# A fixed order at the start of a fused attention and two-FFN kernel: reciprocals, first weight splits and the last unit placed anew

## The chip, the cores and the metric

The kernel runs on one core of one Trainium2 chip. The metric is the device time of one launch in microseconds (us). Before the change the median of three runs is 981.34 us (981.05 to 982.17).

## The reference

Windowed causal attention with a linear bias per head feeds two feed-forward networks, one with a single input matrix, one gated. All arrays are float32. The sequence is 4 x 576 tokens of 8 heads of 64, so 2304 tokens of 512 features.

```python
def _attn_ref(q, k, v):                  # 4 x 8 x 576 x 64
    scores = scale * np.matmul(q, k.transpose(0, 1, 3, 2))
    rel = pos[:, None] - pos[None, :]
    bias = slopes[:, None, None] * (-np.abs(rel))[None]
    mask = (rel >= 0) & (rel < 128)
    scores = np.where(mask, scores + bias[None], -1e9)
    attn = np.exp(scores - scores.max(-1, keepdims=True))
    return np.matmul(attn / (attn.sum(-1, keepdims=True) + 1e-9), v)

def _moe_ref(x, w_in, w_out):            # 512 -> 2048 -> 512
    h = x @ w_in
    return (h / (1.0 + np.exp(-1.702 * h))) @ w_out

def _moe2_ref(x, w_gate, w_val, w_out):  # 512 -> 1536 -> 512
    g = x @ w_gate
    return (g / (1.0 + np.exp(-g)) * (x @ w_val)) @ w_out
```

## The kernel before, in words

The 2304 tokens are 18 tiles of 128. Attention and the first network take them in five blocks of 4, 3, 4, 3 and 4 tiles (`A_BLOCKS`), the second network in five blocks of 4, 4, 4, 4 and 2. This text calls attention on block 0 the front part; it is the only work there is at the start, and the first network can begin on a head pair of block 0 as soon as that pair's output is there.

**Attention on a block** is eight units: four head pairs `hp`, each in two groups `g` of two query tiles. One unit goes through four steps. `scores` multiplies q and k on TensorE into PSUM tiles `sb`; `fold` (VectorE, L223) moves the masked half of the window into place; four sums on VectorE (L268) add the bias and find the row minimum; four exponentials on ScalarE (ACT, L278) also give the row sums. `norm` turns the row sums into reciprocals on VectorE (L291, L292) and multiplies the four tiles by them on GpSimd (POOL, L294). `transposes` turns the four tiles on TensorE (L327), and the result is copied and masked into `pf`: for the units in `ON_VECTOR` by two VectorE products (L339), for the others by a ScalarE copy (L343) and two GpSimd selects (L344, L347). `values`, once per pair, multiplies `pf` with v into the PSUM tile `xb` (L392) and splits the result into a high part `xh` (ScalarE, L410) and a low part `xl` (VectorE, L411). For block 0 extra matmuls without use (`fill`, L186) stand ahead of the transposes.

**The weights** lie in memory as 64-bit floats. `load_w` loads two chunks of 128 x 512 words each (one of `w_in`, one of `w_out`) into one tile, and `split_w` makes a high and a low float32 part of each in six instructions of 128 x 1024 elements: a ScalarE scaling into `cv` (L155), three VectorE operations on bits (L157, L158, L161), a ScalarE rounding into `wt` (L166) and a VectorE subtraction (L167). The pool `cv` has two buffers. There are 16 such pairs for the first network. The first three are split inside the front part; the others are put ahead of the step that needs them.

**The first network** is `h_part(j, f)` (twelve TensorE matmuls, L416 to L418, three for each of the head pairs 0 to 3 in turn; then tanh on ScalarE, a product `th` on VectorE, `gh` on ScalarE and `gl` on VectorE) and `y_part(j, f)` (another twelve). `h_part(0, 0)` needs only the `w_in` chunk of the first weight pair; `y_part(0, 0)` needs the `w_out` chunk. While block 0 goes through ten of the sixteen `f`, attention on block 1 is placed between.

**What sets the order.** Each engine takes its instructions in the order in which they were placed. In the front part that order is written out by hand: a list `ev` of (time, step), sorted by time, whose steps are placed in that order on VectorE, ScalarE, GpSimd and TensorE (`manual_schedule`). The scores of unit h stand at time h, its `norm` at h + `NORM0`, its transposes at h + `TRANSPOSE0`, and `values` of a pair at its second unit + `VALUES0`; the three steps of weight pair i stand at `SPLITS0[i]`, +1 and +2. Everything after the front part is ordered by a scheduler that goes by its own estimate of the times and may place first-network and block 1 work between steps of the front part.

Of the kernel before, what the change touches and what calls it, by code (L numbers as in the profile page):

```python
# [9 lines left out]
F32R = mybir.dt.float32r  # L10
U32 = mybir.dt.uint32
# [5 lines left out]
P = 128  # L17
# [10 lines left out]
B_BLOCKS = (4, 4, 4, 4, 2)  # L28


NORM0, TRANSPOSE0, VALUES0 = 0.6, 2.2, 5.0

ON_VECTOR = (0, 2, 5)

SPLITS0 = (7, 9, 11)

# [10 lines left out]
def attention_two_ffn(ctx: ExitStack, tc: tile.TileContext, q, k, v, w_in, w_out, w_gate, w_val, w_out2, yscr, out):  # L47
# [92 lines left out]
    def load_w(pool, tag, srcs):  # L140

        t = pool.tile([P, 2, 512, 2], U32, tag=tag, name="wraw")
        for i, src in enumerate(srcs):
            nc.sync.dma_start(out=t[:, i].rearrange("p c w -> p (c w)"), in_=src.bitcast(U32))
        return t, pool, tag

    def split_w(raw):


        words, pool, tag = raw  # L150
        low, high = words[:, :, :, 0], words[:, :, :, 1]
        c = cvp.tile([P, 2, 512], U32, tag="cv", name="cv")
        cf = c.bitcast(F32)

        nc.scalar.activation(out=cf, in_=high.bitcast(F32), func=AF.Abs, scale=REBIAS)  # L155
        yield
        nc.vector.tensor_scalar(out=high, in0=high, scalar1=0x80000000, scalar2=None, op0=ALU.bitwise_and)  # L157
        nc.vector.scalar_tensor_tensor(  # L158
            out=low, in0=low, scalar=29, in1=high, op0=ALU.logical_shift_right, op1=ALU.bitwise_or
        )  # L160
        nc.vector.scalar_tensor_tensor(  # L161
            out=c, in0=c, scalar=3, in1=low, op0=ALU.logical_shift_left, op1=ALU.bitwise_or
        )
        yield
        t = pool.tile([P, 2, 2, 512], F32R, tag=tag, name="wt")
        nc.scalar.activation(out=t[:, :, 0, :], in_=cf, func=AF.Copy)  # L166
        nc.vector.tensor_tensor(out=t[:, :, 1, :], in0=cf, in1=t[:, :, 0, :].bitcast(F32), op=ALU.subtract)  # L167
        yield [t[:, 0], t[:, 1]]

# [64 lines left out]
    def scores(j, hp, g):  # L234


        t0, n, lead = span(j)
        u = units[j, hp]
# [24 lines left out]
        for e in range(2):  # L263
            fold([kind(t0 + i) for i in tiles], sb[e][:, : m * 2 * P], quarters)
        for x in range(2 * m):
            e, i = divmod(x, m)
# [18 lines left out]
            )  # L285
        u["prob", g] = prob, stat

    def norm(j, hp, g):
# [4 lines left out]
        for x in range(m):  # L293
            nc.gpsimd.tensor_scalar(  # L294
                out=prob[:, x],
                in0=prob[:, x],
                scalar1=stat[:, 3, x : x + 1],
                scalar2=1.0,
                op0=ALU.mult,
                op1=ALU.mult,  # L300
            )
# [260 lines left out]
    def split_next(w, raw, upto):  # L562
        for i in range(len(w), min(len(raw), upto)):
            w[i] = list(split_w(raw[i]))[-1]

# [5 lines left out]
    for h in range(H):  # L571
        u = 0, h // 2, h % 2
        ev.append((h, lambda u=u: scores(*u)))
        ev.append((h + NORM0, lambda u=u: norm(*u)))
        ev.append((h + TRANSPOSE0, lambda u=u: transposes(*u)))
        if h % 2:
            ev.append((h + VALUES0, lambda u=u: values(*u[:2])))
    for i, at in enumerate(SPLITS0):
        steps = split_w(raw1[i])

        def step(i=i, steps=steps):
            w1[i] = next(steps)

        ev += [(at + s, step) for s in range(3)]
    E = mybir.EngineType
# [10 lines left out]
    def hooks(j, length):  # L596
# [11 lines left out]
        for h in range(H):  # L608
            u = j, h // 2, h % 2
            ev.append((at + step * h, lambda u=u: (scores(*u), norm(*u))))  # L610
            if h % 2 and h < H - 3:
# [100 lines left out]
```

## Time and profile before

| what | value |
|---|---|
| median of three runs | 981.34 us |
| the profiled execution, its own time | 982.34 us |
| its span in the profile | 980.6 us |
| TensorE matmuls busy | 955.4 us (97% of the span) |
| VectorE busy | 474.8 us (48%) |
| ScalarE busy | 343.6 us (35%) |
| GpSimd busy | 145.9 us (15%) |
| chain that ended last: TensorE / VectorE | 87% / 8% |

The page gives busy time per engine over the whole span, the same in 40 slices of about 24.5 us, and the chain of work that ended last. The shares of the whole say little about a change in the first 60 us; those are read from the stretches of the trace, further down. The profiled execution took 1.0 us more than the median of the runs. Where a tile carries the same name in several blocks (`pf`, `xb`, `sb`), the line tells them apart.

### The profile page before, as it was taken

The numbers are of one execution on the slowest core, as the hardware profiler recorded it, in microseconds if no ns is written. First come the engines' busy times: TensorE is split into PE (matmuls) and PEld (weight loads), VectorE is DVE, ScalarE is ACT, GpSimd is POOL, SyncE is SP. The second block draws the span as 40 slices with busy tenths as digits, with TensorE's granted clock in tenths as the row PEclk, the third lists the DMA queues.
The fourth block names the chain that finished last, engine by engine and source line by source line (L and its number), as shares of the span: only waits on it lengthen the run. The fifth ranks groups of instructions, "written<-read, shape, count | busy, mean of one in ns | idle before, by whom it ended". The sixth has DMA issues, their size and how long they took to land.

```text
span 980.6 us, 13815 instructions
## 1 busy us (share of the span) xinstructions
PE 955.4 (97%) x5358; PEld 790.3 (81%) x5358; DVE 474.8 (48%) x1110; ACT 343.6 (35%) x745; POOL 145.9 (15%) x247
## 2 busy tenths in 40 slices
PE   7798899999999999999999999999999999999998
PEld 5465589987777889898888888888888888888897
DVE  6799882545454335536999722232222222322332
ACT  4566542444344334544655411211121111111211
POOL 4326410332122103420000200200020001000000
PEclk9989999999999999999999999999999999999999
DMA  9912230112311112025556200110011000100010
GB/s 337 337 67 65 92 134 22 49 49 62 93 52 53 36 35 71 15 80 189 193 193 222 79 1 1 44 43 1 1 33 43 1 0 12 43 1 1 6 39 22
DMA packets 30881, 69.05 MB, mean 70 GB/s; under 512 B 3424, under 2 KB 11104, under 8 KB 30816
## 3 DMA queue, kind: packets, MB, share of 16 engines
q1 hardware_dynamic: 30816, 68.17, 20.3%
q8 instruction: 42, 0.69, 0.3%
q14 instruction: 23, 0.19, 0.1%
HBM read 57.67 MB, written 10.49 MB: 70 GB/s over the span
## 4 chain that ended last, share of the span: by engine, by line
PE 87%; DVE 8%; ACT 2%; issue 1%; DMA 1%; POOL 1%; ACTq 0%; POOLq 0%; DVEq 0%
PE hp L416 6%; PE y L416 6%; PE y L418 6%; PE y L417 6%; PE hp L418 6%; PE hp L417 6%; PE pg L416 5%; PE pg L418 5%; PE o L526 5%; PE pv L416 5%; PE o L528 5%; PE pv L418 5%; PE pg L417 5%; PE pv L417 5%; PE o L527 5%; PE sb L255 2%
## 5 line engine op out<-in xcount | busy, mean ns | idle before, releaser
L508 DVE SCALAR_TENSOR_TENSOR t<-t,pg 128x512 f32<-128x512 f32 (+1 forms) x60 | 38.1, 634 | 198.1 <-ACT t L507 198.1
L416 PE MATMUL hp<-xh,wt 128*128 128x512 f32 (+1 forms) x320 | 121.7, 380 | 7.9 <-ACT wt L166 6.4
L417 PE MATMUL y<-gl,wt 128*128 128x512 f32 (+1 forms) x320 | 119.5, 373 | 2.8 <-DVE gl L442 2.8
L418 PE MATMUL y<-gh,wt 128*128 128x512 f32 (+1 forms) x320 | 119.4, 374 | 0.0
L418 PE MATMUL hp<-xh,wt 128*128 128x512 f32 (+1 forms) x320 | 119.0, 372 | 0.0
L417 PE MATMUL hp<-xl,wt 128*128 128x512 f32 (+1 forms) x320 | 119.0, 372 | 0.0
L416 PE MATMUL y<-gh,wt 128*128 128x512 f32 (+1 forms) x320 | 114.1, 380 | 0.2
L507 ACT ACTIVATE t<-pg 128x512 f32<-128x512 f32 (+1 forms) x60 | 33.3, 555 | 196.5 <-PE pg L418 196.5
L294 POOL TENSOR_SCALAR prob<-prob,stat 128x128 f32<-128x128 f32 x144 | 68.8, 496 | 202.0 <-DVE stat L292 154.4
L416 PE MATMUL pg<-yh,wt 128*128 128x512 f32 (+1 forms) x240 | 88.8, 370 | 0.0
L416 PE MATMUL pv<-yh,wt 128*128 128x512 f32 (+1 forms) x240 | 88.6, 369 | 0.0
L418 PE MATMUL pg<-yh,wt 128*128 128x512 f32 (+1 forms) x240 | 88.5, 369 | 0.0
L417 PE MATMUL pg<-yl,wt 128*128 128x512 f32 (+1 forms) x240 | 88.4, 368 | 0.0
L418 PE MATMUL pv<-yh,wt 128*128 128x512 f32 (+1 forms) x240 | 88.4, 368 | 0.0
L417 PE MATMUL pv<-yl,wt 128*128 128x512 f32 (+1 forms) x240 | 88.2, 367 | 0.0
L526 PE MATMUL o<-wt,p2h 128*128 128x512 f32 x216 | 84.7, 392 | 0.0
L528 PE MATMUL o<-wt,p2l 128*128 128x512 f32 x216 | 84.3, 391 | 0.0
L527 PE MATMUL o<-wt,p2h 128*128 128x512 f32 x216 | 84.1, 390 | 0.0
L438 DVE SCALAR_TENSOR_TENSOR th<-th,hp 128x512 f32<-128x512 f32 (+1 forms) x80 | 50.3, 631 | 66.3 <-ACT th L437 65.8
L492 POOL TENSOR_TENSOR yl<-yr,yh 128x512 fp32r<-128x512 f32 (+1 forms) x20 | 25.4, 1281 | 376.4 <-ACT yh L491 266.9
L512 ACT ACTIVATE p2h<-t 128x512 fp32r<-128x512 f32 (+1 forms) x60 | 35.3, 588 | 121.0 <-DVE t L511 120.8
L416 PEld LDWEIGHTS hp<-xh,wt 128*128 128x128 f32 x320 | 60.6, 190 | 19.6 <-ACT wt L166 7.5
(80 smaller groups left out, 1663.1 us busy)
## 6 DMA issues: line engine op xcount, KB each, us to landing
wraw<-in_moe_w_out SPq DMA_DIRECT2D x28, 512.0 KB, 5.2
wraw<-in_moe_w_in SPq DMA_DIRECT2D x16, 512.0 KB, 6.7
wraw<-in_moe_w_gate SPq DMA_DIRECT2D x12, 512.0 KB, 4.1
wraw<-in_moe_w_val SPq DMA_DIRECT2D x12, 512.0 KB, 4.6
out<-ob SPq DMA_DIRECT2D x18, 256.0 KB, 2.0
y_scratch<-yt SPq DMA_DIRECT2D x16, 256.0 KB, 2.0
yr<-y_scratch SPq DMA_DIRECT2D x16, 256.0 KB, 2.7
kr<-in_k SPq DMA_DIRECT2D x8, 320.0 KB, 3.2
```

Of the source, the lines that this page charges most:

```text
L294: nc.gpsimd.tensor_scalar(out=prob[:, x], in0=prob[:, x], scalar1=stat[:, 3, x : x + 1], scalar2=1.0, op0=ALU.mult, op1=ALU.mult,)
L416: nc.tensor.matmul(out=out_ap, lhsT=whi, rhs=xhi, start=start, stop=False)
L417: nc.tensor.matmul(out=out_ap, lhsT=whi, rhs=xlo, start=False, stop=False)
L418: nc.tensor.matmul(out=out_ap, lhsT=wlo, rhs=xhi, start=False, stop=stop)
L438: nc.vector.scalar_tensor_tensor(out=th[:, :m], in0=th[:, :m], scalar=1.0, in1=hp[:, :m], op0=ALU.add, op1=ALU.mult)
L492: nc.gpsimd.tensor_tensor(out=yl[:, kk, :m], in0=t[:, :m], in1=yh[:, kk, :m].bitcast(F32), op=ALU.subtract)
L507: nc.scalar.activation(out=th[:, :m], in_=pg[:, :m], func=AF.Tanh, scale=0.5)
L508: nc.vector.scalar_tensor_tensor(out=th[:, :m], in0=th[:, :m], scalar=1.0, in1=pg[:, :m], op0=ALU.add, op1=ALU.mult)
L512: nc.scalar.activation(out=ph[:, :m], in_=th[:, :m], func=AF.Copy)
L526: nc.tensor.matmul(out=o, lhsT=ph[:, c], rhs=w[:, 0, :], start=(f == 0), stop=False)
L527: nc.tensor.matmul(out=o, lhsT=ph[:, c], rhs=w[:, 1, :], start=False, stop=False)
L528: nc.tensor.matmul(out=o, lhsT=pl[:, c], rhs=w[:, 0, :], start=False, stop=(f == NF2 - 1))
```

## The change

Four things change, all of them in the front part.

1. `scores` becomes a generator in two steps: the matmuls and the fold of unit h at time h, its sums and exponentials at h + 0.1. `norm` of unit h moves to h + 1.05, between the two steps of unit h + 1; that of the last unit to 7 + 1.4.
2. The last unit (number 7) is normalised on VectorE instead of GpSimd (`NORM_ON_VECTOR`), and its mask is on VectorE too. In exchange unit 5 goes to ScalarE and GpSimd: `ON_VECTOR` is (0, 2, 7) instead of (0, 2, 5).
3. The weight pair with the tag `w0` (`SINGLES`) is loaded into two tiles of one chunk each, and each chunk is split by instructions of 128 x 512 elements. The tag is used twice, for the first pair of the first network and for the third pair of the second network.
4. `SPLITS0` now gives one time for each of the three steps of every slot.

```diff
-NORM0, TRANSPOSE0, VALUES0 = 0.6, 2.2, 5.0
-ON_VECTOR = (0, 2, 5)
-SPLITS0 = (7, 9, 11)
+TRANSPOSE0, VALUES0 = 2.2, 5.0
+ON_VECTOR, NORM_ON_VECTOR = (0, 2, 7), 7
+SPLITS0 = ((6.5, 8.3, 8.45), (6.6, 9.25, 12.1)), ((8.6, 12.2, 13),), ((12.15, 13.5, 14),)
+SINGLES = ("w0",)
...
+        slots = ((tag, srcs),) if tag not in SINGLES else tuple((f"{tag}.{i}", (src,)) for i, src in enumerate(srcs))
...
-        c = cvp.tile([P, 2, 512], U32, tag="cv", name="cv")
+        c = cvp.tile([P, 2, 512], U32, tag="cv", name="cv")[:, :n]
...
-            nc.gpsimd.tensor_scalar(
+            (nc.vector if j == 0 and 2 * hp + g >= NORM_ON_VECTOR else nc.gpsimd).tensor_scalar(
...
-        ev.append((h, lambda u=u: scores(*u)))
-        ev.append((h + NORM0, lambda u=u: norm(*u)))
+        steps = scores(*u)
+        ev += [(h, lambda steps=steps: next(steps)), (h + 0.1, lambda steps=steps: next(steps))]
+        ev.append((h + (1.05 if h < H - 1 else 1.4), lambda u=u: norm(*u)))
...
-    for i, at in enumerate(SPLITS0):
-        steps = split_w(raw1[i])
-        def step(i=i, steps=steps):
-            w1[i] = next(steps)
-        ev += [(at + s, step) for s in range(3)]
+    for i, times in enumerate(SPLITS0):
+        w1[i] = []
+        for slot, at in zip(raw1[i], times):
+            steps = split_w(slot)
+            def step(i=i, steps=steps):
+                w1[i] += next(steps) or []
+            ev += [(a, step) for a in at]
```

Three places show how the instructions move. The line numbers after the change are 7 to 10 higher.

VectorE at units 0 and 1, before. `stat_163` belongs to unit 0; `sb_190`, `sb_191` and `stat_189` to unit 1.

```order
L268 ISA prob_162,stat_163<-sb_165,bias_68 128x128
L268 ISA stat_163 128x1
L291 TENSOR_SCALAR stat_163<-stat_163 128x4
L292 RECIPROCAL stat_163<-stat_163 128x4
L223 COPY_PREDICATED sb_190<-later_69,sb_190 128x2x128
L223 COPY_PREDICATED sb_191<-later_69,sb_191 128x2x128
L268 ISA prob_188,stat_189<-sb_190,bias_68 128x128
```

The same place after the change. `stat_164` is unit 0's; `sb_185`, `sb_186` and `stat_184` are unit 1's.

```order
L277 ISA prob_163,stat_164<-sb_166,bias_68 128x128
L277 ISA stat_164 128x1
L230 COPY_PREDICATED sb_185<-later_69,sb_185 128x2x128
L230 COPY_PREDICATED sb_186<-later_69,sb_186 128x2x128
L301 TENSOR_SCALAR stat_164<-stat_164 128x4
L302 RECIPROCAL stat_164<-stat_164 128x4
L277 ISA prob_183,stat_184<-sb_185,bias_68 128x128
```

The two reciprocal instructions of unit 0 stand behind the fold of unit 1 instead of ahead of it; so it goes on up to unit 6.

VectorE behind the sums of the last unit, before. The `pf` rows are the masks of unit 5, the first `xl` is that of pair 1, the second that of pair 2.

```order
L339 TENSOR_TENSOR pf<-pt,keep 128x4x128
L339 TENSOR_TENSOR pf<-pt,drop 128x4x128
L291 TENSOR_SCALAR stat<-stat 128x4
L292 RECIPROCAL stat<-stat 128x4
L411 TENSOR_TENSOR xl<-xb,xh 128x512
L157 TENSOR_SCALAR wraw<-wraw 128x1024
L158 SCALAR_TENSOR_TENSOR wraw<-wraw 128x1024
L161 SCALAR_TENSOR_TENSOR cv<-cv,wraw 128x1024
L167 TENSOR_TENSOR wt<-cv,wt 128x2x512
L216 MEMSET sb 64x128
L411 TENSOR_TENSOR xl<-xb,xh 128x512
```

The same place after, from unit 7's reciprocal on (ahead of it stand `xl` of pair 1 and the three bit operations of the first chunk). The `pf` rows are the masks of unit 7, and the `x2` row is `xl` of pairs 2 and 3.

```order
L302 RECIPROCAL stat<-stat 128x4
L304 TENSOR_SCALAR prob<-prob,stat 128x128 x4
L174 TENSOR_TENSOR wt<-cv,wt 128x512
L349 TENSOR_TENSOR pf<-pt,keep 128x4x128
L349 TENSOR_TENSOR pf<-pt,drop 128x4x128
L164 TENSOR_SCALAR wraw<-wraw 128x512
L165 SCALAR_TENSOR_TENSOR wraw<-wraw 128x512
L168 SCALAR_TENSOR_TENSOR cv<-cv,wraw 128x512
L421 TENSOR_TENSOR xl<-xb,xh 128x512 x2
L174 TENSOR_TENSOR wt<-cv,wt 128x512
```

Both halves of the first weight pair and the whole of unit 7 now stand ahead of `xl` of pair 2, and `xl` of pair 3 follows at once, ahead of the second weight pair.

ScalarE at the same place, before. The `prob` rows are the exponentials of units 6 and 7, and the `pf` rows copies of units 4, 6 and 7.

```order
L278 ACTIVATE prob,stat<-prob,stat 128x128 x4
L343 ACTIVATE pf<-pt 128x4x128
L278 ACTIVATE prob,stat<-prob,stat 128x128 x4
L155 ACTIVATE cv<-wraw 128x1024
L410 ACTIVATE xh<-xb 128x512
L343 ACTIVATE pf<-pt 128x4x128
L166 ACTIVATE wt<-cv 128x2x512
```

And after. The `pf` rows are units 4, 5 and 6.

```order
L287 ACTIVATE prob,stat<-prob,stat 128x128 x4
L353 ACTIVATE pf<-pt 128x4x128
L162 ACTIVATE cv<-wraw 128x512 x2
L287 ACTIVATE prob,stat<-prob,stat 128x128 x4
L353 ACTIVATE pf<-pt 128x4x128
L420 ACTIVATE xh<-xb 128x512
L353 ACTIVATE pf<-pt 128x4x128
L173 ACTIVATE wt<-cv 128x512
```

The scaling of both chunks moves ahead of the exponentials of unit 7, and a copy (unit 5) comes between them and `xh` of pair 1.

VectorE at the reciprocals of block 1's last two units, before.

```order
L158 SCALAR_TENSOR_TENSOR wraw<-wraw 128x1024
L167 TENSOR_TENSOR wt<-cv,wt 128x2x512
L291 TENSOR_SCALAR stat<-stat 128x4
L291 TENSOR_SCALAR stat<-stat 128x2
L161 SCALAR_TENSOR_TENSOR cv<-cv,wraw 128x1024
L292 RECIPROCAL stat<-stat 128x4
L292 RECIPROCAL stat<-stat 128x2
L438 SCALAR_TENSOR_TENSOR th<-th,hp 128x512
```

And after.

```order
L302 RECIPROCAL stat<-stat 128x4
L301 TENSOR_SCALAR stat<-stat 128x2
L164 TENSOR_SCALAR wraw<-wraw 128x1024
L168 SCALAR_TENSOR_TENSOR cv<-cv,wraw 128x1024
L302 RECIPROCAL stat<-stat 128x2
L448 SCALAR_TENSOR_TENSOR th<-th,hp 128x512
L165 SCALAR_TENSOR_TENSOR wraw<-wraw 128x1024
L174 TENSOR_TENSOR wt<-cv,wt 128x2x512
```

Over all VectorE rows ahead of the last of these reciprocals, before there are 13 each of L157, L158 and L161 and 12 of L167, all of 128 x 1024. After there are 12, 11, 11 and 10 of that size and two of each in half size. On TensorE the same rows, 412 of them, stand ahead of and up to the last transpose of block 1 before and after.

## Rows read from the trace of the kernel before

**Rows 1.** Stretches: length, busy of PE, PEld, DVE, ACT, POOL, clock, DMA, GB/s.

```profile
0.00:6.12 6.12, 4.54 (x22) 4.14 (x24) 2.13 (x13) 1.28 (x1) 1.46 (x9) 1.00 0.63 197
6.12:31.93 25.81, 21.36 (x148) 13.71 (x146) 19.26 (x108) 14.07 (x63) 12.31 (x31) 1.00 1.02 391
31.93:57.00 25.07, 17.86 (x95) 10.88 (x96) 21.34 (x49) 14.08 (x33) 8.11 (x16) 0.86 0.70 255
57.00:116.77 59.77, 53.33 (x278) 37.61 (x276) 58.88 (x139) 37.24 (x76) 28.53 (x26) 0.91 0.23 69
```

**Rows 2.** Waits of TensorE from 118 us to the end: total, times, longest.

```profile
PE hp L416 <- ACT pf L343: 0.6, 1, 0.6
PE hp L416 <- DVE xl L411: 0.2, 1, 0.2
```

**Rows 3.** Timeline (start, length, instruction [idle before]) at block 1's last units.

```profile
116.56 0.21 DVE L292 RECIPROCAL stat<-stat 128x4 f32<-128x4 f32 x2
...
116.89 2.12 POOL L294 TENSOR_SCALAR prob<-prob,stat 128x128 f32<-128x128 f32 x6 [2.61 <-DVE stat L292]
...
117.32 0.33 PE L327 MATMUL pt<-ident,prob 128*128 128x128 f32 x1 [0.66 <-POOL prob L294]
```

**Rows 4.** Timeline of VectorE in block 0's attention.

```profile
9.31 0.17 DVE L291 TENSOR_SCALAR stat<-stat 128x4 f32<-128x4 f32 x1 [1.08 <-ACT prob L278]
...
24.03 0.08 DVE L268 DVE_READ_ACCUMULATOR2_ANT stat<- 128x1 f32 x1
...
26.22 0.69 DVE L411 TENSOR_TENSOR xl<-xb,xh 128x512 fp32r<-128x512 f32 x1 [0.58 <-ACT xh L410]
...
30.07 0.17 DVE L291 TENSOR_SCALAR stat<-stat 128x4 f32<-128x4 f32 x1 [1.14 <-ACT prob L278]
```

**Rows 5.** Timeline of ScalarE: exponentials of unit 7, scaling, copy, `xh`.

```profile
25.13 0.58 ACT L343 ACTIVATE pf<-pt 128x512 f32<-128x512 f32 x1
25.61 0.58 ACT L410 ACTIVATE xh<-xb 128x512 fp32r<-128x512 f32 x1
...
31.33 0.40 ACT L278 ACTIVATE prob<-prob,stat 128x128 f32<-128x128 f32 x1 [0.82 <-DVE stat L268]
...
32.89 1.13 ACT L155 ACTIVATE cv<-wraw 128x1024 f32<-128x1024 f32 x1
```

**Rows 6.** Timeline of VectorE behind the front part.

```profile
34.53 0.69 DVE L411 TENSOR_TENSOR xl<-xb,xh 128x512 fp32r<-128x512 f32 x1 [0.97 <-ACT xh L410]
35.14 1.18 DVE L157 TENSOR_SCALAR wraw<-wraw 128x1024 uint32<-128x1024 uint32 x1
36.35 1.54 DVE L158 SCALAR_TENSOR_TENSOR wraw<-wraw 128x1024 uint32<-128x1024 uint32 x1
...
43.58 0.68 DVE L157 TENSOR_SCALAR wraw<-wraw 128x1024 uint32<-128x1024 uint32 x1
...
56.10 1.21 DVE L158 SCALAR_TENSOR_TENSOR wraw<-wraw 128x1024 uint32<-128x1024 uint32 x1
57.24 1.21 DVE L167 TENSOR_TENSOR wt<-cv,wt 128x1024 fp32r<-128x1024 f32 x1
```

**Rows 7.** Timeline of TensorE: `values` of pairs 2 and 3, first `hp`, later `hp`.

```profile
35.49 2.17 PE L392 MATMUL xb<-pf,qkv 128*64 128x256 f32 x20
40.29 0.80 PE L416 MATMUL hp<-xh,wt 128*128 128x512 f32 x1 [2.63 <-ACT wt L166]
```

**Rows 8.** VectorE groups by form, 0 to 120 us: busy, mean ns, idle before.

```profile
L442 DVE TENSOR_TENSOR gl<-th,gh 128x512 fp32r<-128x512 f32 x7 | 4.7, 677 | 0.0
...
L115 DVE TENSOR_SCALAR bias<-rel 128x128 bf16<-128x128 f32 x8 | 1.2, 221 | 0.0
...
L108 DVE TENSOR_SCALAR later<-rel 128x128 f32<-128x128 f32 x1 | 0.3, 294 | 0.1
```

**Rows 9.** Stretches around the second fall of TensorE's clock.

```profile
53.90:57.30 3.40, 1.36 (x6) 0.59 (x4) 3.40 (x7) 3.06 (x8) 2.16 (x4) 1.00 0.01 2
57.30:60.70 3.40, 3.40 (x24) 2.73 (x24) 3.40 (x6) 2.54 (x4) 0.26 (x1) 0.50 0.01 2
```

More of the change, by code (lines that the diff above doesn't have):

```diff
@@ L140, in load_w @@
     def load_w(pool, tag, srcs):
[L142 to L145, printed above, removed]
+        slots = ((tag, srcs),) if tag not in SINGLES else tuple((f"{tag}.{i}", (src,)) for i, src in enumerate(srcs))
+        raws = []
+        for tag, srcs in slots:
+            t = pool.tile([P, len(srcs), 512, 2], U32, tag=tag, name="wraw")
+            for i, src in enumerate(srcs):
+                nc.sync.dma_start(out=t[:, i].rearrange("p c w -> p (c w)"), in_=src.bitcast(U32))
+            raws.append((t, pool, tag))
+        return raws
     def split_w(raw):
         words, pool, tag = raw
+        n = words.shape[1]
         low, high = words[:, :, :, 0], words[:, :, :, 1]
-        c = cvp.tile([P, 2, 512], U32, tag="cv", name="cv")
+        c = cvp.tile([P, 2, 512], U32, tag="cv", name="cv")[:, :n]
         cf = c.bitcast(F32)
@@ L164, in split_w @@
         yield
-        t = pool.tile([P, 2, 2, 512], F32R, tag=tag, name="wt")
+        t = pool.tile([P, n, 2, 512], F32R, tag=tag, name="wt")
         nc.scalar.activation(out=t[:, :, 0, :], in_=cf, func=AF.Copy)
         nc.vector.tensor_tensor(out=t[:, :, 1, :], in0=cf, in1=t[:, :, 0, :].bitcast(F32), op=ALU.subtract)
-        yield [t[:, 0], t[:, 1]]
+        yield [t[:, i] for i in range(n)]
     def w1_src(i):
@@ L264, in scores @@
             fold([kind(t0 + i) for i in tiles], sb[e][:, : m * 2 * P], quarters)
+        yield
         for x in range(2 * m):
@@ L286, in scores @@
         u["prob", g] = prob, stat
+        yield
     def norm(j, hp, g):
@@ L563, in split_next @@
         for i in range(len(w), min(len(raw), upto)):
-            w[i] = list(split_w(raw[i]))[-1]
+            w[i] = [chunk for slot in raw[i] for chunk in list(split_w(slot))[-1]]
     for hp in range(H // 2):
@@ L609, in hooks @@
             u = j, h // 2, h % 2
-            ev.append((at + step * h, lambda u=u: (scores(*u), norm(*u))))
+            ev.append((at + step * h, lambda u=u: (list(scores(*u)), norm(*u))))
             if h % 2 and h < H - 3:
```

## Prediction

> **What bounds the kernel now.** I read first where TensorE stops waiting. From 118 us to the end it waits twice, 0.6 and 0.2 us [rows 2], so whatever shifts its work up to there shifts the end by as much. Its last long waits before that end at 117.32, with the transposes of block 1's last units: they waited for GpSimd's six multiplications, which waited for two reciprocals on VectorE, done at 116.77 [rows 3]. The order puts the same 412 TensorE rows up to the last transpose of block 1 before and after, so the work that is left behind is the same. Then I read VectorE up to 116.77, by stretches [rows 1]. It is busy 2.13 + 19.26 + 21.34 + 58.88 = 101.61 us and idle 15.16: 3.99 before the first scores (to 6.12), 6.55 in the front part (6.12 to 31.93, the end of the last unit's sums), 3.73 from there to 57, and 0.89 in the last 59.77. TensorE in that last stretch is busy 53.33 of 59.77, part of it at a clock share below 1 (mean 0.91), so it has room and VectorE has none. So the last reciprocal of block 1 is a sum of two things, the VectorE work that stands ahead of it and the VectorE idle ahead of it, and I cost the change as the change of these two.
>
> **The work ahead of the last reciprocal.** (a) By the order, three instructions of 128 x 1024 no longer stand ahead of it: one L158, one L161, one L167, if two halves count as one. Such an instruction is followed by the next 1.14 us after its start (56.10 to 57.24) [rows 6], so 3 x 1.14 = 3.4 us less. They are only put off: the weights they make belong to a later f of the first network, and VectorE has free time once TensorE sets the pace. (b) Unit 7's four multiplications come to VectorE. No row of before shows that operation there. The nearest from below is L115, one input, 128 wide, 0.221 us; from above L108, 0.294 us with a float32 result [rows 8]. I take 4 x 0.22 = +0.9 (0.6, if the starts are closer than the lengths, to 1.3). That GpSimd loses them gains nothing here, since nothing but unit 7 waits. The masks change places between units 5 and 7, two L339 each, at no net cost. (c) Four VectorE instructions of 1024 become eight of 512. Two of 512 take 2 x 0.677 = 1.35 [rows 8] where one of 1024 takes 1.21 [rows 6], so +0.15 each, +0.6 (0.2 to 0.6). (d) The first weight pair's L157 and L158 took 1.18 and 1.54 where later ones take 0.68 and 1.21 [rows 6], 0.8 more, while GpSimd normalised and masked. The first chunk will still meet GpSimd's masks of units 5 and 6, the second will not: -0.4 (-0.8 to 0). Sum: -3.4 + 0.9 + 0.6 - 0.4 = **-2.3**.
>
> The Trainium skill ("GPSIMD Engine Reference", Key points) says that GpSimd shares its SBUF interfaces with VectorE and contends with VectorE instructions in a two-port mode or with two SBUF inputs; it speaks against moving unit 5's masks to GpSimd beside the first chunk. By it (d) would be 0 and the forecast 0.4 later; the trace agrees as far as the 1.18 against 0.68 goes.
>
> **Idle in the front part.** The 6.55 are six waits, first 1.08, last 1.14 us [rows 4], 5.99 in all, and 0.56 of small gaps. Five are waits for the exponentials, ahead of a reciprocal; the reciprocal now stands behind the next unit's fold. The fold of an even unit takes 1.15 to 1.2 and covers a wait of 1.1; that of an odd one takes 0.64 and leaves about 0.5. Unit 0's and unit 6's waits so become 0.5, unit 1's and 3's vanish. Pair 0's `xl` is not helped: it starts 2.2 us after the sums of unit 5 (24.03 to 26.22) [rows 4], because ScalarE has the exponentials, a copy and `xh` to do [rows 5], in the same order after. VectorE did unit 5's reciprocals in that time and now does not, so 2.2 idle stay. Left are 0.5 + 2.2 + 0.5 + 0.56 = 3.8, so **-2.7** (-3.2 to -2.0). The last sums end at 29.2 instead of 31.93.
>
> **Idle behind it.** Here the new order adds two waits. First, `xl` of pair 1. Counted back from 29.2 (0.84 for the sums, 0.5 wait, 0.3 reciprocals, 0.64 fold, 0.84 sums) unit 6's sums start at 26.1 and its exponentials run from 26.4 to 28.0 (1.6 per unit, 31.33 to 32.89) [rows 5]. In ScalarE's queue then stand a copy (0.5), two half scalings (1.15 for both, by the 1.13 of the whole), the exponentials of unit 7, a copy and `xh` (0.5 each): 28.0 + 0.5 + 1.15 + 1.6 + 0.5 + 0.5 = 32.25, and `xl` starts at 32.35. That is 2.2 ahead of before (34.53 [rows 6]), but VectorE waits 3.1 for it. Queued behind are the first chunk, unit 7's norm and the whole split. Second, `xl` of pair 3. VectorE goes on at 32.95 with the first half (1.55 + 0.2 for GpSimd), reciprocals 0.3, norm 0.9, half `wt` 0.6, masks 1.2, second half 1.55, `xl` of pair 2 0.6, done at 39.85. TensorE turns unit 7 by 36.2, does `values` of pair 2 and the first two of pair 3 in 2.17 [rows 7] (38.4), then, by the order, six `hp` and one pair of scores (about 1.95 at 0.23 each and a few gaps, 40.3), and only then the rest of `values` (1.4, 41.7). ScalarE's `xh` makes it 42.4, and `xl` of pair 3 starts at 42.5: a wait of 2.65. But TensorE sits idle for some 3 us ahead of unit 7. After a stretch with 1.36 of 3.40 us busy its clock fell from 2.4 to 1.2 GHz (share 1.00, then 0.50) and it did 3.4 us of work at half rate [rows 9], which lost 1.7 us. If that happens here the wait is 4.35. I take 3.5, the middle. With 0.3 of small gaps the 3.73 of before become 6.9, so **+3.2** (+2.3 to +5.2). At the end, 0.89 may grow if VectorE now and then comes before TensorE has the input: **+0.2** (-0.3 to +2.5).
>
> TensorE's own start gains: the first `hp` at 38.4 instead of 40.29 [rows 7]. That hides nothing more, since it waits for the second weight pair anyway. On SP only two tags of the same loads change, and the first weights are loaded far ahead of 28 us. The second network's split in halves adds about 0.6 to a VectorE that is half busy over the span, and TensorE does not wait there [rows 2]: nothing, and 0.6 if that cover were gone.
>
> **The sum.** -2.3 - 2.7 + 3.2 + 0.2 = -1.6 us. The profiled execution took 982.34 us around a span of 980.6, so it would take 980.7; the median of the runs is 1.0 lower, and 981.34 - 1.6 gives **979.7 us**. With all bounds together: -3.4 - 3.2 + 2.3 - 0.3 = -4.6, and -1.5 - 2.0 + 5.2 + 2.5 = +4.2. I take 0.2% (1.96 us) as what a measurement of this kernel can tell from no change.
>
> **Rivals.** (1) Slower: TensorE sets the pace of the tail. Unit 7's turn, `values` and the first `hp` run at 1.2 GHz, and on VectorE first `xl` of pair 3 and then `th` of the first `hp` head the queue, so each us of TensorE's lateness is a us of VectorE idle, with the second and third weight pairs behind. Price: +0.85 for the wait of 4.35 instead of 3.5, +2.4 for twelve `hp` at 0.43 instead of 0.23, and +0.9 for half of one more stretch at half rate at the wait for the second weights: -1.6 + 4.15 = +2.55, 983.9 us. It decides as soon as TensorE is more than 1.6 us later than I have it. For it speaks that rows 9 show the fall; against it that the chain gives this stretch to VectorE. The Trainium skill ("TensorE: Matmul & The Clock Gate", What's actually happening) says that the throttled state is the default and that activity releases it; by it the fall ahead of unit 7 is likely, and the trace agrees (1.36 busy of 3.40 us, then 0.50). (2) Faster: the clock holds at 2.4 GHz in the tail (wait 2.65, -0.85) and the first chunk does not collide with GpSimd (-0.4), and the last stretch's small waits vanish (-0.5): -3.3, 978.0 us. For it speaks that short waits in the front part cost no clock (share 1.00) [rows 1]. (3) No gain: the lead is there at 57, but TensorE, 53.33 of 59.77 busy, cannot follow, and VectorE idles until TensorE has its inputs: 0 to -0.6, 981.0 us. Against it speaks the clock share of 0.91 in that stretch, which leaves TensorE room.
>
> **Chances.** The forecast's own case 0.42 (978.3 to 981.1, and about 4 in 10 of it beyond 0.2%), rival 1 0.16, rival 2 0.25, rival 3 0.17. Faster by over 0.2%: 0.42 x 0.4 + 0.25 x 0.95 + a little = 0.42. Slower by over 0.2%: 0.16 x 0.75 = 0.12. Within: 0.46. The range for 8 in 10 is 976.9 to 982.9; the forecast's own is 978.3 to 981.1.
>
> **What the profile will show.** Right: the sums of unit 7 end near 29.2; no wait over 0.6 ahead of a reciprocal in block 0 but for the one at pair 0's `xl` (about 2.2); a VectorE wait of about 3 before `xl` of pair 1 and of 2.6 to 4.4 before that of pair 3; the last reciprocals of block 1 near 115; TensorE's clock at 0.50 once between 33 and 42. Wrong: if VectorE idles over 2 us between 57 and 115 (rival 3), if `th` of the first `hp` is waited for (rival 1), or if TensorE waits somewhere behind block 1's last transpose.

## The result, and the profile after

The changed kernel takes **990.14 us** (median of four runs, 989.42 to 991.47) against 981.75 of the kernel before beside it: ratio 1.0084, 95% interval 1.0071 to 1.0097. I had predicted 979.7 us and a range up to 982.9; the change is slower by 8.4 us. The profiled execution took 990.1 us around a span of 988.4; the span is 7.8 us longer than before. TensorE's matmuls are busy 959.3 us of it, against 955.4 before, for the same work: so about half of the 7.8 us is more idle time on TensorE and half is work done slower (mean granted clock 0.983 against 0.990).

The stretches of after, for [rows 1] (length, busy of PE, PEld, DVE, ACT, POOL, clock, DMA, GB/s):

```profile
0.00:6.12 6.12, 4.54 (x22) 4.14 (x24) 2.13 (x13) 1.28 (x1) 1.45 (x9) 1.00 0.66 188
6.12:31.93 25.81, 22.82 (x150) 15.67 (x148) 18.91 (x107) 15.93 (x69) 13.33 (x34) 0.87 1.02 394
31.93:57.00 25.07, 17.39 (x90) 9.93 (x90) 19.72 (x47) 11.33 (x23) 3.34 (x5) 0.81 0.71 254
57.00:116.77 59.77, 52.38 (x283) 37.50 (x281) 55.34 (x141) 36.60 (x78) 29.32 (x30) 0.94 0.22 70
```

VectorE idles 4.43 us in the last of these stretches (59.77 - 55.34), where it idled 0.89 before; from there to its last reciprocal, at 119.62, it is busy throughout. The timeline of VectorE behind the front part, for [rows 6]:

```profile
33.15 0.69 DVE L421 TENSOR_TENSOR xl<-xb,xh 128x512 fp32r<-128x512 f32 x1 [2.94 <-ACT xh L420]
33.75 0.57 DVE L164 TENSOR_SCALAR wraw<-wraw 128x512 uint32<-128x512 uint32 x1
34.36 1.00 DVE L165 SCALAR_TENSOR_TENSOR wraw<-wraw 128x512 uint32<-128x512 uint32 x1
...
36.32 0.16 DVE L301 TENSOR_SCALAR stat<-stat 128x4 f32<-128x4 f32 x1
...
39.84 0.69 DVE L165 SCALAR_TENSOR_TENSOR wraw<-wraw 128x512 uint32<-128x512 uint32 x1
...
45.70 0.69 DVE L421 TENSOR_TENSOR xl<-xb,xh 128x512 fp32r<-128x512 f32 x1 [3.23 <-ACT xh L420]
...
49.30 0.67 DVE L448 SCALAR_TENSOR_TENSOR th<-th,hp 128x512 f32<-128x512 f32 x1
...
78.55 0.69 DVE L448 SCALAR_TENSOR_TENSOR th<-th,hp 128x512 f32<-128x512 f32 x1 [1.25 <-ACT th L447]
...
107.24 0.23 DVE L230 COPY_PREDICATED sb<-later,sb 128x64 f32<-128x64 uint32 x1 [2.45 <-PE sb L263]
...
117.46 0.16 DVE L302 RECIPROCAL stat<-stat 128x4 f32<-128x4 f32 x1
...
119.47 0.15 DVE L302 RECIPROCAL stat<-stat 128x2 f32<-128x2 f32 x1
```

The two new waits (2.94 and 3.23 us) are there, and block 1's last reciprocals end at 117.62 and 119.62, not near 115 (116.77 before, [rows 3]). Most of the idle time behind 57 us is the wait of 2.45 us for scores of block 1. TensorE's timeline at unit 7, ahead of these scores, and at block 1's last units, where [rows 3] had a wait of 0.66:

```profile
37.06 1.08 PE L337 MATMUL pt<-ident,prob 128*128 128x128 f32 x4 [3.74 <-DVE prob L304]
38.08 3.45 PE L402 MATMUL xb<-pf,qkv 128*64 128x256 f32 x20
...
98.05 1.17 PE L337 MATMUL pt<-ident,prob 128*128 128x128 f32 x3 [1.32 <-POOL prob L304]
100.30 0.47 PE L337 MATMUL pt<-ident,prob 128*128 128x128 f32 x1 [1.08 <-POOL prob L304]
...
106.65 0.54 PE L263 MATMUL sb<-kr,qr 64*64 64x192 f32 x4
...
119.84 0.48 PE L337 MATMUL pt<-ident,prob 128*128 128x128 f32 x1 [2.68 <-POOL prob L304]
...
126.96 0.44 PE L337 MATMUL pt<-ident,prob 128*128 128x128 f32 x2
```

TensorE's clock is at its lower level from 98.8 to 105.6 us, and the twelve `hp` matmuls between the second wait and the scores start 0.43 us apart instead of 0.23. The last of block 1's transposes in the kernel before, which no row ahead shows:

```profile
123.14 0.44 PE L327 MATMUL pt<-ident,prob 128*128 128x128 f32 x2
```

And the waits of TensorE from 118 us to the end, for [rows 2] (total, times, longest):

```profile
PE pt L337 <- POOL prob L304: 2.7, 1, 2.7
PE y L426 <- ACT gh L451: 1.2, 1, 1.2
PE y L427 <- DVE gl L452: 0.6, 1, 0.6
PE hp L426 <- ACT pf L353: 0.6, 1, 0.6
```

The middle two are new: TensorE is starved again behind block 1. The timeline of ScalarE there shows by what:

```profile
136.06 0.62 ACT L451 ACTIVATE gh<-th 128x512 fp32r<-128x512 f32 x1
140.91 1.12 ACT L162 ACTIVATE cv<-wraw 128x1024 f32<-128x1024 f32 x1 [4.23 <-DMA wraw<-in_moe_w_out]
141.93 1.05 ACT L173 ACTIVATE wt<-cv 128x1024 fp32r<-128x1024 f32 x1
143.24 0.90 ACT L447 ACTIVATE th<-hp 128x384 f32<-128x384 f32 x2 [0.25 <-PE hp L428]
146.44 1.06 ACT L173 ACTIVATE wt<-cv 128x1024 fp32r<-128x1024 f32 x1 [2.31 <-DVE cv L168]
147.41 1.09 ACT L451 ACTIVATE gh<-th 128x384 fp32r<-128x384 f32 x2
```

The last weight pair (number 15) is loaded when `values` of block 1 frees its place, and lands at 140.9. ScalarE's queue holds `gh` of steps 0 and 1 of block 1 behind that pair's rounding, which waits for VectorE to go through the pair's bits; TensorE reaches `y` and waits.

### The profile page after: what moved, and what is told of

It is laid out like the page before. It is cut to its first block, busy times and chain, and to the rows that moved or that the text cites. A ratio compares the mean times of both kernels' runs of the same rounds, so it can differ in the third digit from the quotient of the medians.

```text
span 988.4 us, 13816 instructions
## 1 busy us (share of the span) xinstructions
PE 959.3 (97%) x5358; PEld 793.6 (80%) x5358; DVE 475.7 (48%) x1122; ACT 343.8 (35%) x749; POOL 150.0 (15%) x243
## 4 chain that ended last, share of the span: by engine, by line
PE 89%; DVE 5%; ACT 2%; POOL 2%; DMA 1%; issue 1%; SPq 0%; ACTq 0%; DVEq 0%; POOLq 0%
PE y L428 6%; PE y L427 6%; PE hp L426 6%; PE y L426 6%; PE hp L428 6%; PE hp L427 6%; PE pg L426 5%; PE pg L428 5%; PE o L536 5%; PE pv L426 5%; PE o L538 5%; PE pv L428 5%; PE pg L427 5%; PE pv L427 5%; PE o L537 5%; PE sb L263 2%
## 5 line engine op out<-in xcount | busy, mean ns | idle before, releaser
L426 PE MATMUL hp<-xh,wt 128*128 128x512 f32 (+1 forms) x320 | 123.0, 385 | 5.9 <-ACT wt L173 4.8
L428 PE MATMUL hp<-xh,wt 128*128 128x512 f32 (+1 forms) x320 | 120.6, 377 | 0.0
L304 POOL TENSOR_SCALAR prob<-prob,stat 128x128 f32<-128x128 f32 x140 | 66.5, 492 | 215.2 <-DVE stat L302 134.6
```

The lines of the kernel that those rows point to most:

```text
L304: (nc.vector if j == 0 and 2 * hp + g >= NORM_ON_VECTOR else nc.gpsimd).tensor_scalar(out=prob[:, x], in0=prob[:, x], scalar1=stat[:, 3, x ...
L426: nc.tensor.matmul(out=out_ap, lhsT=whi, rhs=xhi, start=start, stop=False)
L428: nc.tensor.matmul(out=out_ap, lhsT=wlo, rhs=xhi, start=False, stop=stop)
```

## The experiments

Three theories. **Tail** (rival 1, widened): the late unit 7 and the wait for `xl` of pair 3 make the loss. **Order** (called layout in the expectations): the scheduler lays out everything behind the front part by its own estimate, any change alters that, and the loss arises there. It gives wide ranges, so a time inside one says little for it. **GpSimd**: work beside VectorE is slowed.

To compare kernels I use TensorE's **lost time**: the length of a stretch minus busy time times clock, from the view by stretches. TensorE's work is the same in all of them, but for the extra matmuls without use, and from 160 us on all idle alike (4.1 to 5.4 us). The measure is rough, since it takes the mean clock of a whole stretch: the spans less the three losses lie between 949.5 and 954.3 us, so differences of 2 us say little. (The 19.6 and 14.8 in one expectation below are summed over finer slices; the table has 18.5 and 14.7 for the same.) The last column is TensorE's wait for GpSimd's multiplied tiles (`pt` for `prob`) from 57 to 132 us. Each ratio is to runs of the kernel before beside it, whose medians lie between 981.3 and 982.2. All in us.

| kernel | median | ratio to before, interval | lost 0-57 | 57-130 | 130-160 | wait |
|---|---|---|---|---|---|---|
| before | 981.75 | | 15.9 | 11.6 | 0.0 | 2.0 |
| after | 990.14 | 1.0084 (1.0071-1.0097) | 18.5 | 15.1 | 3.4 | 6.8 |
| after_again | 990.44 | 1.0077 (1.0063-1.0091) | 18.2 | 15.2 | 3.4 | 7.0 |
| after_nudge | 985.95 | 1.0046 (1.0031-1.0061) | 18.2 | 10.4 | 3.5 | 7.0 |
| after_lag | 980.13 | 0.9983 (0.9973-0.9992) | 18.3 | 8.9 | 0.0 | 5.6 |
| front_new_lag36 | 987.06 | 1.0054 (1.0037-1.0071) | 18.5 | 14.4 | 0.0 | 9.4 |
| gl_first | 983.49 | 1.0017 (1.0006-1.0028) | 16.7 | 14.1 | 0.0 | 7.0 |
| nudge_fill | 982.53 | 1.0006 (0.9996-1.0015) | 15.8 | 12.6 | 0.0 | 4.7 |
| front_old_lag42 | 981.95 | 1.0002 (0.9992-1.0011) | 17.3 | 11.4 | 0.2 | 3.3 |
| front_old_lag36 | 984.01 | 1.0022 (1.0012-1.0031) | 17.3 | 12.8 | 0.1 | 7.9 |
| recip_only | 987.92 | 1.0065 (1.0048-1.0082) | 17.3 | 20.0 | 0.0 | 3.5 |
| recip_kept | 975.75 | 0.9939 (0.9925-0.9954) | 14.3 | 8.9 | 0.0 | 3.0 |
| unit7_only | 985.68 | 1.0044 (1.0029-1.0059) | 17.2 | 14.2 | 0.3 | 6.5 |
| split_only | 976.63 | 0.9952 (0.9937-0.9966) | 18.4 | 5.7 | 0.0 | 3.2 |
| no_unit7_early | 980.01 | 0.9986 (0.9975-0.9996) | 13.8 | 12.8 | 0.6 | 3.4 |
| xl3_later | 982.39 | 1.0005 (0.9995-1.0016) | 15.2 | 12.3 | 0.0 | 5.9 |
| norm7_early | 980.34 | 0.9992 (0.9980-1.0003) | 14.7 | 10.2 | 0.6 | 3.8 |
| norm7_xl3 | 987.08 | 1.0058 (1.0043-1.0073) | 16.2 | 11.3 | 4.4 | 6.9 |
| norm7_lag36 | 989.17 | 1.0083 (1.0070-1.0096) | 14.9 | 21.0 | 0.0 | 11.0 |
| fill_unit7 | 983.37 | 1.0021 (1.0010-1.0031) | 16.3 | 10.9 | 0.6 | 4.9 |

### The parts alone

**recip_only** and **recip_kept** differ in one number:

```diff
 # old ON_VECTOR and SPLITS0 times, no SINGLES
-ev.append((h + 0.6, norm))
+ev.append((h + (1.05 if h < H - 1 else 1.4), norm))   # recip_only
+ev.append((h + (1.05 if h < H - 1 else 0.6), norm))   # recip_kept
```

> The kernel before with only the first part of the change: the reciprocals behind the next unit's fold. Three theories of the loss of 8.4 us. Tail: it is the wait of 3.2 us of VectorE for xl of pair 3, with the second and third weight pairs queued behind it, and what TensorE then does late. Layout: the scheduler that orders everything behind the front part lays it out anew for any change, and the loss arises there. GpSimd: VectorE is slowed by GpSimd's work put beside it. By tail and by GpSimd: the second weight pair stays between xl of pairs 2 and 3, so nothing of the loss appears, and the front part gains about 2 us: 979 to 982. By layout: 984 to 988, although the last unit's sums end about 2 us sooner than before (31.93).

> The kernel before with the reciprocals of units 0 to 6 behind the next unit's fold, and those of the last unit at 7.6, where they were (recip_only had them at 8.4, behind the first weight pair's bit operations). By the tail theory recip_only's loss was that one place: here the last unit's transposes start near 32.5 (34.23 before), and the front part's 2 us arrive at the end: 978.5 to 981. By layout: 977 to 987 without a tie to the front part, with the difference made between 57 and 150 us.

recip_only: 987.92; its last unit's reciprocals fell behind the first pair's bit operations, and TensorE waited 4.6 us for that unit. recip_kept: **975.75**, 6 us faster than before and faster than forecast. Its last sums end at 28.6 instead of 31.93, and by 57 us it has lost 1.6 us less. The rest of the 6 us is won behind, which the tail theory doesn't give; the order theory's range began at 977 and missed it too.

**unit7_only** (`ON_VECTOR, NORM_ON_VECTOR = (0, 2, 7), 7` alone) and **split_only** (`SINGLES` and the new `SPLITS0` alone):

> The kernel before with only the last unit normalised and masked on VectorE (and unit 5 masked on GpSimd). By tail: 0.9 us more VectorE work and no new wait at xl of pair 3, since the second weight pair stands ahead of it: 981.5 to 983.5. By GpSimd: the three bit operations of the first weight pair take about 1.6 times as long beside the masks of units 5 and 6, 982.5 to 985. By layout: 984 to 988, with waits of TensorE behind 60 us that the kernel before does not have.

> The kernel before with only the first weight pair in two chunks and the new times of the weight steps. By tail: the second weight pair stands behind xl of pair 3 here too, so a good part of the loss appears: 984 to 988, with the second pair's third bit operation near 49 us (before 45.95). By layout: 984 to 988 too, but with the second pair no later than before and TensorE late only behind 60 us. By GpSimd: 981 to 983, as units 5 and 7 are masked as before. If the three parts add up, the three kernels' differences sum to about 8.4 us.

unit7_only: 985.68, with most of its loss behind 57 us: as the order theory had it, not the tail. split_only: **976.63**, where all three theories had it no faster. The three parts sum to +6.6 + 4.4 - 4.7 = +6.3 with recip_only, and to -6.2 with recip_kept (-5.9) in its place. They don't add up to anything that can be read as the worth of a part.

### Mending the tail

**xl3_later**, **norm7_early** and both together (**norm7_xl3**):

```diff
-SPLITS0 = ..., ((8.6, 12.2, 13),), ...
+SPLITS0 = ..., ((8.6, 11.9, 13),), ...                # xl3_later
-ev.append((h + (1.05 if h < H - 1 else 1.4), norm))
+ev.append((h + (1.05 if h < H - 1 else 0.95), norm))  # norm7_early
```

> The changed kernel with one time altered: the middle step of the second weight pair at 11.9 instead of 12.2, so that its three bit operations stand ahead of xl of pair 3 on VectorE. By tail: the wait of 3.2 us is filled with work, the second pair's third bit operation ends near 46 instead of 51.1, and 3 to 5 us come back: 985 to 987.5. By layout and by GpSimd: the wait may go, but the time stays at 988.5 to 991.

> The changed kernel with one time altered: the last unit's reciprocals and multiplications at 7.95 instead of 8.4, so ahead of xl of pair 1 and of the first chunk's bit operations on VectorE. Tail theory, made narrower by the runs so far: the loss begins where the last unit stands behind the first chunk, so that TensorE idles 3.74 us ahead of its transposes, loses its clock, does the values late, and VectorE waits 3.2 us for xl of pair 3. By it the transposes start near 33.5 instead of 37.06, that idle time goes, the wait for xl of pair 3 falls below 1 us, and the time is 980 to 984. Layout theory (the order that the scheduler makes behind the front part decides): the same signs up to 50 us, but 986 to 991.

> The changed kernel with both times altered: the last unit's reciprocals at 7.95, and the second weight pair's middle step at 11.9. Tail theory: each of the two removes the same wait at xl of pair 3, so they don't add: 979 to 982, near norm7_early's 980.3. Had they separate causes, both gains would come: about 973. By layout anything from 975 to 987.

xl3_later gave 982.39 and norm7_early 980.34, 7.8 and 9.8 us back (for the first the tail theory had 3 to 5), and in norm7_early unit 7's transposes start at 31.56 and the lost time by 57 falls from 18.5 to 14.7. That looked like the tail theory proved. But both together took 987.08: the tail is mended twice, and the loss is back, between 130 and 160 us (4.4), with a wait of 2.8 us of `y` for `gh`. The theory that had looked best failed here.

**no_unit7_early** (after with the last unit as before, reciprocals at 7.6) and **fill_unit7** (14 matmuls without use ahead of unit 7's transposes instead of 3):

> The changed kernel with the last unit as before: reciprocals at 7.6, multiplications and mask on GpSimd, unit 5's mask on VectorE; so split_only (976.6) with the reciprocals of units 0 to 6 behind the next fold. By the tail theory the gain of the reciprocals comes on top: 973.5 to 976. By layout: 976 to 985.

> The changed kernel with 14 instead of 3 of the matmuls without use ahead of the last unit's transposes, so that TensorE is busy for most of the 3.74 us in which it idles there. If the clock's fall at 37.3 us is what costs: the clock stays at 1.00 there, values takes 2.2 instead of 3.45 us, xl of pair 3 comes 1.3 us sooner, and the time is 986 to 988.5. If it is the lateness of unit 7 itself: VectorE still waits 2 us or more at xl of pair 3, and the time stays at 988.5 to 991.

no_unit7_early: 980.01, above both recip_kept and split_only, whose edits it joins, though it has the least lost time by 57 us of all (13.8). fill_unit7: 983.37, better than either theory had it. Each got one sign: the clock stays at 1.00 from 31 to 44 us and `values` takes 2.17 us, but VectorE still waits 3.17 us ahead of `xl` of pair 3, now for scores. Its order behind the front part differs as well, so it doesn't tell the two apart.

### The same front part, another order behind it

**after_lag**, **front_new_lag36** (changed front part), **front_old_lag42**, **front_old_lag36** (old front part) and **norm7_lag36** (norm7_early's) alter one number, which acts on block 1 and later only:

```diff
-SPREAD, LOAD_LAG, TRANSPOSE_LAG, VALUES_LAG = 0.65, 0.3, 4.0, 3.0
+SPREAD, LOAD_LAG, TRANSPOSE_LAG, VALUES_LAG = 0.65, 0.3, 4.2, 3.0   # or 3.6
```

> The changed kernel with one number altered that acts only behind the front part: block 1's transposes are placed a little later (4.2 steps behind the scores instead of 4.0). VectorE's rows are the same for the first 170, so to about 58 us, and differ from there on. Tail theory: unit 7's transposes at 37, the wait of 3.2 us for xl of pair 3 and the second weights at 51 all stay, and so does the time: 988.5 to 991.5. Layout theory: the changed kernel's 990 is one draw of many layouts, and another layout behind the same front part gives 979 to 987.

> The changed kernel with block 1's transposes at 3.6; its front part is that of the changed kernel row for row. Layout theory: 977 to 990, with unit 7 late and the wait of 3.2 us for xl of pair 3 as in the changed kernel whatever the time is. Tail theory: 988 to 991.5, and 6 us or more above front_old_lag36.

> The kernel before with block 1's transposes at 4.2 instead of 4.0, so the front part of before with another order behind it; after_lag is the changed front part with the same number. Layout theory: the times of each front part spread by 5 us or more over the numbers, and the two front parts differ by less than that; this one lies anywhere from 976 to 987. Tail theory: 980 to 983, and at each number the changed front part is the slower by 5 us or more.

> The kernel before with block 1's transposes at 3.6. Layout theory: 976 to 987. Tail theory: 980 to 983.

> The changed kernel with the last unit's reciprocals at 7.95, and block 1's transposes at 3.6. At this number the front part of before took 984.0 and the changed one 987.1. If the late unit 7 costs whatever the order behind it is, mending it gives about as much here as the TensorE time lost up to 57 us says (19.6 against 14.8 us, so 4 to 5 us): 981 to 983.5. If only the order behind decides, anything from 977 to 988.

after_lag decides against the tail. Its wait for `xl` of pair 3 is 3.21 us, its lost time by 57 us 18.3, all as in after, and it takes **980.13**. The stretches of after, after_lag and norm7_lag36 (columns as above):

```profile
0.00:57.00 57.00, 44.75 (x259) 29.75 (x260) 40.76 (x167) 28.54 (x92) 18.12 (x47) 0.86 0.85 310
57.00:130.00 73.00, 62.93 (x329) 44.66 (x328) 66.46 (x156) 43.85 (x88) 40.67 (x40) 0.92 0.21 67
130.00:160.00 30.00, 28.25 (x144) 24.89 (x143) 19.75 (x26) 12.19 (x19) 1.33 (x1) 0.94 0.30 109
```

```profile
0.00:57.00 57.00, 44.96 (x258) 29.82 (x259) 40.43 (x165) 28.55 (x92) 18.23 (x47) 0.86 0.84 309
57.00:130.00 73.00, 64.70 (x363) 45.50 (x362) 71.18 (x162) 46.33 (x92) 41.83 (x40) 0.99 0.24 80
130.00:160.00 30.00, 30.00 (x167) 28.95 (x166) 17.36 (x25) 11.67 (x20) 0.00 (x0) 1.00 0.23 81
```

```profile
57.00:130.00 73.00, 59.13 (x285) 40.13 (x285) 61.49 (x145) 39.50 (x82) 33.63 (x34) 0.88 0.22 70
```

The first lines of after and after_lag agree; TensorE's busy time and clock differ in the second and third. norm7_lag36 has the mended front part and yet took 989.17, above both forecasts and 2.1 us above front_new_lag36, the unmended one under the same number. Over the four orders that were run for each (as it was, one fill more, 4.2, 3.6), the old front part took 981.8, 982.5, 982.0 and 984.0, the changed one 990.1, 986.0, 980.1 and 987.1: 3.3 us more in the mean, with differences from -1.8 to +8.4. By 57 us the changed one has lost more in all four (1.0 to 2.6 us by the table). Whether that arrives at the end stays open; that the changed front part makes 8.4 us whatever stands behind it is refuted. The order theory missed here as well: it had each front part spread by 5 us or more, and the old one spreads by 2.3, the changed one by 10.0.

**nudge_fill** (before) and **after_nudge** (after) have `FILL = 7, 3` instead of `6, 3`:

> The kernel before with 7 instead of 6 of the matmuls without use at the very start. The order of the front part is the same, row for row; the order behind it differs, since the scheduler estimates one matmul more. By the tail theory 981.3, within 1 us. By layout it differs by 2 us or more, to either side, and the difference is made behind 57 us.

> The changed kernel with 7 instead of 6 of the matmuls without use at the very start; its rows stand in the same order up to about 150 us on every engine but TensorE, where few differ. It shows what a repetition is worth. Both theories: 989 to 991.5, with the wait for the last weights at 136 to 141 us again. If the clock's fall at 10 us in the front part, which the profiled execution of the changed kernel had and those of two kernels with the same rows up to there had not, comes and goes between executions, it is absent here in some of them: 987 to 989 and a wider spread.

> The changed kernel itself, once more. Other kernels of this study show two or three levels of time some 3 us apart, each with its own mean clock (0.989 and 0.992 for the kernel with the last weight pair pinned), and the changed kernel has shown only 0.983 to 0.985 so far. If the clock's fall at 10 us in the front part comes and goes between executions, some executions here lie near 987 with a clock near 0.987, the others near 990; if it belongs to this order, all lie at 989 to 991.5.

nudge_fill: +0.9, within the 1 us of the tail theory and under the 2 us of the order theory. after_nudge is the surprise: 985.95, 4.2 us under after and below every forecast, though the order of its VectorE, ScalarE and GpSimd rows is the same throughout, and TensorE's but for a few scores of block 1 at 43 to 47 us. Two stretches of it, around and behind two waits for GpSimd's tiles that end at 97.4 and 99.7 us (1.33 and 1.23 us):

```profile
98.60:102.00 3.40, 2.33 (x11) 1.95 (x12) 3.37 (x7) 1.91 (x3) 2.31 (x3) 1.00 0.00 0
102.00:105.40 3.40, 3.40 (x18) 2.33 (x17) 3.31 (x11) 2.04 (x4) 2.96 (x3) 1.00 0.00 0
```

The same stretches in after, where the two waits end at 98.1 and 100.3 us (1.32 and 1.08 us):

```profile
98.60:102.00 3.40, 2.30 (x7) 1.60 (x7) 3.37 (x7) 1.61 (x3) 2.16 (x3) 0.52 0.00 0
102.00:105.40 3.40, 3.40 (x10) 2.63 (x9) 2.79 (x5) 0.80 (x1) 3.40 (x4) 0.50 0.00 0
```

The same waits, and TensorE's clock falls to 1.2 GHz in one and not in the other. From 57 to 130 both are busy 62.6 to 62.9 us, at a clock of 1.00 in after_nudge and 0.92 in after. In after_nudge VectorE does not wait for the scores behind these stretches, its last reciprocal ends at 116.60 instead of 119.62 (116.77 before), and the last transposes of block 1, which after has at 126.96, start at:

```profile
122.95 0.44 PE L337 MATMUL pt<-ident,prob 128*128 128x128 f32 x2
```

That is where the kernel before had them (123.14). So about half of after's 8.4 us is clock, under one order; the other half comes behind block 1, where after_nudge loses 3.5 us as after does. It isn't shown that the one matmul holds the clock: after_again, which is after unaltered, has executions at 986.24 (mean clock 0.991), 988.41 (0.988) and four at 990.3 to 991.0 (0.983 to 0.984).

### The last weight pair

**gl_first** pins pair 15 behind `gl` of block 1's step 1; the rest of VectorE's, ScalarE's and GpSimd's rows is as in after:

```diff
...
+steps = split_w(slot)                       # pair 15 only
+next(steps)
+with tc.issue_after(gl_ins[1, 1].ins):      # bit operations queued behind that gl
+    next(steps)
+w[i] = next(steps)
```

> The changed kernel with one pair's order pinned and no other row moved on VectorE, ScalarE and GpSimd up to there: the bit operations, rounding and subtraction of the last weight pair (number 15), which wait for a load that lands at 140.9 us, stand behind gl of step 1 of block 1 instead of ahead of its gh. Layout theory, first part: TensorE's waits for gh and gl at 148 to 150 us (1.75 us) and the fall of its clock behind them (1.7 us lost) go, and nothing else: 986 to 987.5, 3.5 us less than the changed kernel. If those waits only moved a loss that is there anyway, 989 to 991.

ScalarE in gl_first, beside the rows of after above:

```profile
138.90 1.14 ACT L162 ACTIVATE cv<-wraw 128x1024 f32<-128x1024 f32 x1 [4.05 <-DMA wraw<-in_moe_w_out]
...
142.74 0.53 ACT L453 ACTIVATE gh<-th 128x384 fp32r<-128x384 f32 x1 [0.49 <-DVE th L450]
...
148.54 1.06 ACT L173 ACTIVATE wt<-cv 128x1024 fp32r<-128x1024 f32 x1 [0.97 <-DVE cv L168]
```

`gh` no longer waits for the pair, TensorE's waits for `gh` and `gl` are gone, and the lost time from 130 to 160 us falls from 3.4 to 0.0. This part of the loss is shown. With the 4.2 us of after_nudge it makes 7.6 of the 8.4 us; no run has both alterations, so that they add is arithmetic. The median of gl_first fell by 6.7 us, 3 more than its 3.4; the profiled execution had no clock fall at 10 us in the front part, which after's had (lost by 57: 16.7 against 18.5), and its ten runs spread from 981.4 to 985.7.

## Why the prediction was wrong, point by point

- **The work ahead of the last reciprocal** was right. VectorE's busy time up to 119.62 is 96.10 (the four stretches) and 2.85 more, 98.95, against 101.61: -2.7, predicted -2.3. That the sum came so close is in part luck: `gl` took 5.5 us for seven instead of 4.7, which no term had, and the weight instructions fell by more than was forecast (57.5 to 53.2 by their groups, -4.3 instead of -3.2). Within it (d) failed: beside GpSimd's masks the first chunk's three operations took 2.57 us from start to start (33.75 to 36.32), not 1.75. The Trainium skill ("GPSIMD Engine Reference", Key points) says that GpSimd shares its SBUF interfaces with VectorE and contends with instructions that have two SBUF inputs. The trace agrees: L165 took 1.00 beside the masks, and 0.69 for the second chunk.
- **Idle up to 57 us** was predicted +0.5 (-2.7 + 3.2) and came out as +2.0 (idle of 6.90 and 5.35 against 6.55 and 3.73). Both waits were sized well (2.94 for 3.1, 3.23 for 3.5), and the clock fell at unit 7 as expected. What I had not counted is a fall at 10 us (granted clock 0.50 from 10.0 to 16.8), behind which VectorE waited 1.68 us for scores at 17.44: the last sums end at 30.2, not at 29.2. The profiled execution of gl_first, with the same rows up to there, does not have it, and its sums end at 28.1; so without the fall the front part would have gained 1.1 us more than forecast.
- **Idle behind 57 us** is the term that failed: +0.2 (-0.3 to +2.5) predicted, +3.5 measured (4.43 against 0.89). The last reciprocal came 2.85 us later, not 1.6 sooner. The step that failed is "it has room and VectorE has none": I took TensorE's 53.33 busy of 59.77 us as room and the stretch as given, VectorE full and TensorE following. In after the clock fell at 98.8, between two waits for GpSimd's tiles, the scores of block 1 came late at half rate, and VectorE waited 2.45 us for them; 1.25 more went to a `th` at 78.55. after_nudge, with the same order on VectorE, ScalarE and GpSimd and the clock at 1.00 there, has no such wait for scores. Where the order changes too, the runs put the time behind 57 anywhere from 5.7 to 21.0 us of TensorE's lost time, and the times follow it on the whole: the seven kernels below 982 us lost 5.7 to 13.4 us behind 57, the eight above 985 13.9 to 21.0; ahead of 57 the two groups overlap, 13.8 to 18.4 and 14.9 to 18.5.
- **"TensorE waits twice behind block 1, 0.6 and 0.2 us"** was read from before and carried over. That was the second step that failed: the end did not shift by what block 1 shifted by. Block 1's last transposes end at 127.40, 3.8 us later than before (123.58); of the 4.0 us that are still missing, about 3.4 are the place of pair 15 (gl_first). The prediction named this as what would make it wrong. The order of ScalarE showed it ahead of any run: `gh` behind a rounding that hangs on a load.
- **Rival 1** had the side right, at 983.9, but not the reason. Its own sign, `th` of the first `hp` waited for, did not come (49.30, no wait), and after_lag has its whole mechanism and no loss. Rival 2 did not happen. **Rival 3** gave its sign: VectorE idled 3.70 us between 57 and 115 (1.25 and 2.45), most of it for TensorE's scores. At 57 little of the lead was left (58.19 us of VectorE work to the last reciprocal, 58.88 before), and what I held against this rival, the room that a clock share of 0.91 leaves, was the wrong reading: under half rate TensorE was the later one.
- **The channel.** Behind 57 us the wait that differs most is TensorE's for GpSimd's tiles: 2.0 us before, 6.8 after, 3.0 to 5.6 in the kernels below 981, 6.5 to 11.0 in the slow ones but for recip_only. No run took GpSimd out of block 1, so this is a correlation and not shown as the cause; after_nudge has 7.0 and the clock held.

## What to carry to other kernels

Where a scheduler lays out the work behind an edit, one run before and one after compare two draws of an order; run each with two or three small alterations that don't touch the edit, and read the spread, before a part of the edit is praised or blamed. Read the new order behind the edit too: look at every load that lands late for what is queued behind its first user on each engine. And where the rows agree but the times don't, compare the granted clock before the order is blamed. Two of the change's parts are worth trying under more orders: the reciprocals of units 0 to 6 behind the next fold (recip_kept, 975.75), and the chunks with their times (split_only, 976.63). Each was faster than both kernels under the one order that it was run with; joined, they took 980.01.

## What the runs showed of the hardware

- The clock of TensorE can fall or hold after the same waits: 0.52 against 1.00 at 98.6 to 102.0 us, after waits that agree to 0.15 us. The median is 4.2 us lower where it held. It held in the kernel with one more matmul without use at the start, but the unaltered kernel's executions, too, range from 986.24 us (mean clock 0.991) to 991.47 (0.984). The Trainium skill ("TensorE: Matmul & The Clock Gate", What's actually happening) says that the watch on activity runs freely and isn't reset when a kernel starts. The traces agree so far: the clock falls in one kernel and holds in the other after the same waits; no run varies the moment of the start alone.
- A GpSimd multiplication of 128x128 took 372 ns in the front part of after (28 of them) and 952 ns from 57 to 132 us (24), while VectorE worked through the weights. No run separates the two engines there.
